# Softmax denominators of two head quads taken together, merged rows moved once a set, and later planned landings, in a scheduled transformer block

## The chip, the cores and the metric

One core of a Trainium2 chip runs the whole kernel. Times are device microseconds of that core, from unprofiled executions; the profile is of one further execution with the hardware profiler on. Engines are named as the profile names them: PE is TensorE (PEld its weight loads), DVE VectorE, ACT ScalarE, POOL GpSimd, SP SyncE, whose queue issues nearly all transfers.

## What is computed

A transformer block with conditioning: layer norm and modulation, attention with 32 heads of 16 dimensions over 2048 tokens, a residual, a second layer norm, and a GEGLU feed-forward network (FFN) with 1792 hidden columns.

```python
sa, ca, ga, sb, cb, gb = split(silu(c) @ w_mod, 6)        # six rows of 512
h = layernorm(x) * (1 + ca) + sa                          # x: 2048 x 512
q, k, v = heads(h @ wqkv)                                 # 32 heads of 16
p = softmax(q @ k.T * 16 ** -0.5)                         # 32 x 2048 x 2048
x = x + ga * (merge(p @ v) @ wo)
h = layernorm(x) * (1 + cb) + sb
x = x + gb * ((gelu(h @ w_gate) * (h @ w_up)) @ w_down)
```

## The kernel before

**Tiling.** The 2048 queries are cut into nine sets (`SETS`): seven of 256 rows and two of 128. The 32 heads are cut into eight quads of four. A unit is a quad with a set (the first two sets go together in the first four quads, the last two in their first four). For each unit the scores of four heads against all keys are made on TensorE in blocks of 128 x 512 in PSUM; ScalarE takes their exponential two or three blocks at a time (`E<-ps_sc`), and VectorE takes some of the blocks instead, by a bit trick (`dreg`, `kq`, `mreg`, `sq`). The weighted sums with V accumulate in `ps_pv`; V has one column of ones more, so the 17th row of each head is the softmax denominator.

**Denominators (`unit_end`).** When a unit's sums are complete, VectorE copies them to `osb`, one of four slots of 256 columns. Then a chain runs: a transfer gathers the four rows of denominators on 128 partitions (`den<-osb`), VectorE takes the reciprocal (`rden<-den`), a transfer stores it in DRAM (`scr_rec<-rden`), four transfers broadcast it to the partitions of the four heads (`rb<-scr_rec`), and VectorE multiplies (`onorm<-osb,rb`). A head fills 16 of the 32 partitions that its place in the quad has. For some pairs of quads (`MERGED`), four transfers then move the rows of the odd quad beside those of the even one (`onorm<-onorm`), so that one matmul of the output projection takes both. The quads 6 and 7 of the last two sets (and quad 5 of the last) take another way, over TensorE (`near_end`).

**The rest of the work.** Projections of later rows, the output projection (`side_wo`), the second layer norm and the FFN of sets that are done (`side_ffn`) are side work: `plan` gives each piece a start and a due position in the sequence of score blocks, and `stream` doles it out in proportion. The FFN's weights are loaded again for each of the first sets, in pieces of 256 KB through two buffers for the gate and up weights (names beginning with `st`; the down weights of those sets `sd`), and kept for the last ones (`wg`, `wu`, `wd`).

**What sets the order.** The program's order on each engine is fixed when it is built. `stream` walks through the score blocks with a model of each engine's time and picks at each step what the model takes to be ready. Engines then run in that order, so a wrong estimate shows as a wait in which everything behind it on the same engine stands. For a transfer the model takes an issue cost on SyncE (`ISSUE`, by the first letters of the transfer's name) and a landing time, to which `MARGIN` adds some nanoseconds: `db` is the gather, `dc` the store, `dd` the broadcasts, `de` the merges, `qo` the transfers that split queries of odd and even quads.

**Fillers.** When TensorE would be idle, `stream` puts in matmuls that have no use (`xs,ident`), if the columns that it streamed in the last 3413 ns are fewer than `FILL` (`short`):

```python
    def short(self, t):
        w = 0
        for s, k in reversed(self.log):
            if s < t - 3413:
                break
            w += k
        return FILL - w
```

**The tail.** After the last exponential (`tail`) come the projection and FFN of the last two sets.

Of the kernel before, what the change touches and what calls it, by code (L numbers as in the profile page):

```python
# [6 lines left out]
ALU = mybir.AluOpType  # L7
# [6 lines left out]
P = 128  # L14
# [3 lines left out]
DH = 16  # L18
# [4 lines left out]
NKT = S_TOK // P  # L23
VW = DH + 1
EPS = 1e-5
FILL = 4200
GELU_C = 0.044715
TANH_C0 = float(np.sqrt(2.0 / np.pi))

# [2 lines left out]
NSETS = len(SETS)  # L32
OCOL = (0, 256, 0, 256, 0, 256, 0, 256, 384)
# [15 lines left out]
FLOW = sum(a + n <= 1536 for a, n in SETS)  # L49
URGENT = 9  # L50
LATE = 2
ISSUE = {"dd": 462, "de": 630, "db": 610, "dc": 400, "st": 410, "sd": 530, "wu": 420, "wg": 510, "wd": 480, "ou": 400}
MARGIN = {"db": 1200, "dd": 1200, "de": 1200}
BACK = 6
GAP = 120
END = (0, None)
# [30 lines left out]
class _Recorder:  # L87
# [289 lines left out]
    def bn_aggr(self, out, in_):  # L377
        return self.rec("dve", lambda e: e.bn_aggr(out, in_), [in_], [out], cost=99)

    def dma(self, eng, out, in_, sem, noncontig=False):  # L380
        def fn(e):
            if noncontig:
                with self.nc.allow_non_contiguous_dma(reason="small strided transfer"):
                    return e.dma_start(out, in_)
            return e.dma_start(out, in_)  # L385
        n = mybir.dt.size(out.dtype)
        for _, k in out.ap:
            n *= int(k)
        run = min(int(a.ap[-1][1]) * mybir.dt.size(a.dtype) for a in (out, in_))
        return self.rec(eng, fn, [in_], [out], dma=sem, cost=(n, run, MARGIN.get(sem[:2], 0)))  # L390

    def emit(self, final):
        for s in self.count:
# [34 lines left out]
class _Kernel(_Recorder):  # L428
# [845 lines left out]
    def plan(self, ends, nsplit, begin):  # L1274

        def at(i):
            return i * 2.5 if i < nsplit / 2.5 else nsplit + 3 * (i - nsplit / 2.5)
        a = ends[0] + 33
        w = [(self.side_first, 0, at(30))]
        w.append((self.side_wo_load, at(30), at(30)))  # L1280
        w.append((lambda: self.side_dc(1), at(30), at(51)))
        w.append((self.side_mod, at(50), at(59)))
        w.append((self.scale_wo, at(59), at(59)))
        b, c = begin[2] - 12, begin[3] - 12
        w.append((lambda: self.side_dc(2), at(59), b))
        w.append((lambda: self.side_dc(3), b, c))
        for g in range(1, 4):
            w.append((lambda g=g: self.side_q_all(g), c + (a - c) * (g - 1) // 3, c + (a - c) * g // 3))
        n = ends[-1]
        m = NSETS - 2  # L1290
        for k in range(m):
            s0 = ends[k] + 33
            e = ends[m] - (20)
            if k < m - 1:
                e = max(ends[k + 1] + 30, ends[0] + 33 + (e - ends[0] - 33) * sum(SETS[k]) // SETS[m][0])
            w.append((lambda k=k: self.side_wo(k), s0, min(e, s0 + 15 * SETS[k][1] // P)))
            if k < m - 1:
                w.append((lambda k=k: self.side_ffn(k), s0, e))
            else:
                w.append((lambda k=k: self.turns(self.before_last(m), self.side_ffn(k)), s0, e))  # L1300
        k, s0 = NSETS - 2, ends[-2] - 16
        w.append((lambda: self.either(self.side_ffn(k, True), self.near_end(k + 1, 6, lambda: self.spare[2]), self.wo_last(k + 1), self.tail_rest(k, self.mi[:, :])), s0, n - 20))
        res = []
        for mk, s, e in w:
            self.dry = True
            tot = sum(y[0] for y in mk() if y is not None)
            self.dry = False
            res.append([mk(), s, e, tot, None])
        return res
# [31 lines left out]

    def short(self, t):

        w = 0
        for s, k in reversed(self.log):
            if s < t - 3413:
                break
            w += k
        return FILL - w

    def stream(self):
        self.split = True
# [8 lines left out]
        m = NSETS - 2  # L1361
# [9 lines left out]
        ends = [0] * NSETS  # L1371
# [13 lines left out]
        for u in units[2:]:  # L1385
            n, kpb = NKT * u[3] // 512, 512 // u[3]
            plain = list(range(T0 // kpb))
            m = len(plain) * 2 // 3
            for r in plain[:m] + list(range(len(plain), n)) + plain[m:]:
                add(u, r)  # L1390
        nseq = len(seq)
# [6 lines left out]
        pos = c = e = rp = loaded = 0  # L1398
# [28 lines left out]
        def pv(rnd, i, src):  # L1427
            u, r, g0 = rnd
            self.require([("v", r * (512 // u[3]) // 4, u[1] // 2)])
            self.pv_mms(rnd, acc_of(u), src, i, u not in begun, left[u] == 1)  # L1430
# [8 lines left out]
        def pv_next():  # L1439

            res = []
            for k in open_rounds():
                rnd = rounds[k]
                u, r, g0 = rnd
                if group[u] != cg or any(g0 + j not in self.slot for j in range(4)) or len(res) == 2:
                    break
                if left[u] == 1 and self.blocked(u):
                    break
                src = [self.slot[g0 + j] for j in range(4)]
                if ("v", r * (512 // u[3]) // 4, u[1] // 2) not in self.have:  # L1450
                    if tq is not None:
                        break
                    x = 0.0
                else:
                    x = self.probe(lambda: pv(rnd, 0, src))
                if res:
                    x = max(x, res[0][0])
                res.append((x, 0, k, rnd, 0, src, None))
                if left[u] <= 2:
                    break  # L1460
            n = 0
            for q in wait:
                u = q["rnd"][0]
                if group[u] != cg:
                    break
                for i, src in q["ready"]:
                    if n == 2 or (left[u] == 1 and self.blocked(u)) or (res and left[u] <= 2):
                        break
                    n += 1
                    res.append((self.probe(lambda: pv(q["rnd"], i, src)), 1, i, q["rnd"], i, src, q))  # L1470
            res.sort(key=lambda x: (max(x[0], t + 30), x[1]))
            return res

# [26 lines left out]
        while cg <= group[units[-1]]:  # L1500
# [7 lines left out]
            t = max(self.pe_now(), virt)  # L1508
# [168 lines left out]
    def unit_end(self, u, acc):  # L1677
        sets, qd, q0, W = u
        b, lo, hi = self.osb_span(u)
        osb, rb = self.osb[:, lo:hi], self.rb[:, lo:hi]  # L1680
        assert not self.blocked(u)
        self.copy("dve", osb, acc[:, 0:W])
        if sets[0] >= NSETS - 2 and len(sets) == 1 and qd >= (6 if sets[0] == NSETS - 2 else 5):
            self.done(("osb", sets[0], qd))
            return
        self.live[u] = (lo, hi)
        m = 4 * W // P
        o = 8 if BCOL[sets[0]] else 0
        sem = b + 4 * (o > 0)
        pair = (qd - 1, qd) in self.merged(sets[0])  # L1690
        s2 = self.scr2[b, P * o:P * o + 4 * W]
        den, rden = self.den[:, b, o:o + m], self.rden[:, b, o:o + m]
        steps = [
            ("sp", lambda: self.dma("sp", den, self.osb[DH:P:32, lo:hi].rearrange("j (a n) -> j a n", n=m), "db%d" % sem)),
            lambda: self.recip(rden, den),
            ("sp", lambda: self.dma("sp", s2.rearrange("(p n) -> p n", p=P), rden, "dc%d" % sem)),
            ]
        steps += [("sp", lambda j=j: self.dma(
            "sp", self.rb[32 * j:32 * j + DH, lo:hi],
            s2[W * j:W * j + W].rearrange("(o n) -> o n", o=1).broadcast_to([DH, W]), "dd%d%d" % (sem, j)))  # L1700
            for j in range(4)]

        def fin2():
            c = OCOL[sets[0]]
            self.tt("dve", self.onorm[:, qd, c:c + W], osb, rb, ALU.mult)
            if self.probing is None:
                self.live.pop(u)
                self.done(("half", u))
                if not pair:
                    for k in sets:  # L1710
                        self.done(("onorm", k, qd))

        def merge(j):
            c = OCOL[sets[0]]
            self.dma("sp", self.onorm[32 * j + DH:32 * j + 2 * DH, qd - 1, c:c + W], self.onorm[32 * j:32 * j + DH, qd, c:c + W],
                     "de%d%d" % (qd // 2, j))
            if self.probing is None and j == 3:
                for k in sets:
                    self.done(("onorm", k, qd))

        def free():
            c = OCOL[sets[0]]
            return ("den", u) in self.have and all(
                ("wo", k) in self.have for k in range(sets[0]) if OCOL[k] < c + W and c < OCOL[k] + SETS[k][1])
        self.task(steps, ("den", u))
        self.task([fin2], ("norm", u), free)
        if pair:
            self.task([("sp", lambda j=j: merge(j)) for j in range(4)], None,
                      self.after([("half", u)] + [("onorm", k, qd - 1) for k in sets]))


    def tail(self, ka, kb):

# [217 lines left out]
```

## Time and profile before

| | us |
|---|---|
| median of 3 runs | 832.73 (832.40 to 832.94) |
| the profiled execution | 841.73 |
| its span, first to last instruction | 840.0 |
| TensorE busy | 763.9 |
| VectorE busy | 727.4 |
| ScalarE busy | 793.3 |

The profiled execution is 9.0 us longer than the median. In the views that follow, a group's line gives line, engine, operation, the tiles written and read, shapes and count, then busy time, the mean of one in ns, and the idle time before it with what ended it. A line of the waits gives the total, the count and the longest. A line of the windows gives the stretch and its length, then for each engine shown the busy time and the count of instructions, then the granted TensorE clock, the share of the DMA engines and GB/s. A line of the timeline gives start and length, and in brackets the idle time before it. A line on a transfer of SyncE gives min, median and max of the issuing instruction in ns; one on transfers by size gives count, KB each and us to landing.

### The profile page before, as it was taken

What the parts mean: (1) busy time and instruction counts of PE and PEld (TensorE: products, weight loads), DVE (VectorE), ACT (ScalarE), POOL (GpSimd) and SP (SyncE); (2) the same over time, 40 slices, a digit from 0 to 9 for tenths busy, and PEclk for the clock granted to TensorE, in tenths of its full rate; (3) what the DMA queues carried; (4) which work ended last, traced back from release to release, by engine and by line L of the source; (5) the groups of instructions that cost most, each with busy time, mean ns of one, the idle gap of its engine ahead of it and who ended that gap; (6) DMA issues with size and microseconds to landing.
All of it is one profiled execution on the core that took longest, in us unless ns stands there. A gap on an engine that the chain in (4) does not pass through costs nothing.

```text
span 840.0 us, 37609 instructions
## 1 busy us (share of the span) xinstructions
PE 763.9 (91%) x17153; PEld 369.8 (44%) x17157; DVE 727.4 (87%) x1504; ACT 793.3 (94%) x746; POOL 4.5 (1%) x12
## 2 busy tenths in 40 slices
PE   8889999998899898989899899998998899999898
PEld 4333334343443354434444454344443443346567
DVE  7754878989899998899999998999997999989764
ACT  6999999999899998999999999999998999999782
POOL 1000000000000000000000000000000000000000
PEclk9999999999999999999999999999999999999899
DMA  9100000012540045114410541043234522200000
GB/s 303 44 14 11 12 9 18 8 23 72 148 133 23 11 135 139 32 28 126 134 42 17 148 125 39 16 124 111 59 86 114 166 73 65 64 12 11 14 13 13
DMA packets 105708, 57.40 MB, mean 68 GB/s; under 512 B 26701, under 2 KB 104782, under 8 KB 105550
## 3 DMA queue, kind: packets, MB, share of 16 engines
q1 hardware_dynamic: 105020, 54.48, 23.7%
q8 instruction: 134, 2.20, 1.1%
q10 hardware_dynamic: 530, 0.53, 0.2%
q14 instruction: 24, 0.20, 0.1%
HBM read 50.04 MB, written 2.35 MB: 62 GB/s over the span
## 4 chain that ended last, share of the span: by engine, by line
ACT 72%; PE 15%; DVE 5%; DMA 5%; SPq 2%; issue 1%; DVEq 0%
ACT E L335 70%; PE ps_sc L322 6%; PE ps_mi L322 6%; PE ps_pv L322 3%; SPq L385 2%; ACT wreg L335 2%; DMA scr_rec<-rden 2%; DMA rb<-scr_rec 2%; DVE mreg L347 1%; DMA xs<-in_B_w_down_dram 1%; DMA mreg<-in_B_w_gate_dram 1%; DVE wreg L339 0%; DMA mreg<-in_B_w_up_dram 0%; DVE wreg L356 0%; DVE onorm L339 0%
## 5 line engine op out<-in xcount | busy, mean ns | idle before, releaser
L335 ACT ACTIVATE E<-ps_sc 128x1024 bf16<-128x1024 f32 (+2 forms) x700 | 768.1, 1343 | 32.0 <-PE ps_sc L322 31.7
L322 PE MATMUL ps_sc<-qT,kT 32*128 32x256 bf16 (+3 forms) x2048 | 199.3, 275 | 25.5 <-ACT E L335 20.6
L322 PE MATMUL ps_sc<-qo,kT 32*128 32x256 bf16 (+2 forms) x2048 | 201.2, 275 | 19.5 <-ACT E L335 16.9
L322 PE MATMUL ps_pv<-E,vaug 128*17 128x256 bf16 (+2 forms) x3232 | 157.7, 275 | 1.9 <-DVE osb L356 1.2
L347 DVE TENSOR_SCALAR dreg<-ps_sc 128x512 uint16<-128x512 f32 x192 | 130.3, 685 | 15.4 <-PE ps_sc L322 13.7
L322 PE MATMUL ps_mi<-wreg,mreg 128*32 128x256 bf16 x2816 | 120.2, 279 | 7.3 <-DMA mreg<-in_B_w_up_dram 2.2
L322 PEld LDWEIGHTS ps_sc<-qT,kT 32*128 32x128 bf16 (+1 forms) x2048 | 61.3, 92 | 120.7 <-ACT E L335 100.3
L322 PEld LDWEIGHTS ps_sc<-qo,kT 32*128 32x128 bf16 x2048 | 61.5, 92 | 111.8 <-ACT E L335 99.1
L322 PEld LDWEIGHTS ps_pv<-E,vaug 128*17 128x17 bf16 x3232 | 61.8, 90 | 59.9 <-issue 41.8
L322 PEld LDWEIGHTS ps_mi<-wreg,mreg 128*32 128x32 bf16 x2816 | 65.0, 97 | 46.8 <-issue 24.2
L322 PE MATMUL ps_pv<-mreg,vs 128*17 128x256 bf16 (+2 forms) x1796 | 80.4, 272 | 3.5 <-DVE mreg L347 3.2
L347 DVE TENSOR_SCALAR mreg<-dreg 128x2048 uint16<-128x2048 uint16 x120 | 79.7, 681 | 0.1
L347 DVE TENSOR_SCALAR mreg<-ps_sc 128x512 uint16<-128x512 f32 x96 | 65.1, 685 | 8.7 <-PE ps_sc L322 7.9
L347 DVE TENSOR_SCALAR kq<-ps_sc 128x512 uint16<-128x512 f32 x96 | 65.2, 684 | 8.5 <-PE ps_sc L322 7.7
L322 PEld LDWEIGHTS ps_pv<-mreg,vs 128*17 128x17 bf16 x1796 | 39.4, 91 | 19.4 <-issue 6.9
L322 PE MATMUL ps_mi<-hreg,wreg 128*32 128x512 bf16 (+1 forms) x496 | 37.9, 377 | 1.0 <-DVE vaug L356 0.6
L352 DVE SCALAR_TENSOR_TENSOR wreg<-wreg,ps_mi 128x512 bf16<-128x512 bf16 x49 | 33.3, 679 | 3.3 <-PE ps_mi L322 2.6
L356 DVE CAST wreg<-ps_mi 128x512 bf16<-128x512 f32 x49 | 33.5, 684 | 1.9 <-PE ps_mi L322 1.0
L339 DVE TENSOR_TENSOR wreg<-wreg 128x1024 bf16<-128x1024 bf16 (+1 forms) x56 | 34.3, 613 | 0.0
L347 DVE TENSOR_SCALAR mreg<-kq 128x2048 uint16<-128x2048 uint16 x48 | 32.4, 684 | 0.7 <-PE ps_pv L322 0.7
L347 DVE TENSOR_SCALAR mreg<-mreg 128x2048 uint16<-128x2048 uint16 x48 | 32.6, 679 | 0.0
L339 DVE TENSOR_TENSOR onorm<-osb,rb 128x256 bf16<-128x256 f32 (+2 forms) x59 | 25.2, 428 | 6.1 <-DMA rb<-scr_rec 6.0
(171 smaller groups left out, 725.3 us busy)
## 6 DMA issues: line engine op xcount, KB each, us to landing
mreg<-in_B_w_up_dram SPq DMA_DIRECT2D x46, 256.0 KB, 3.1
mreg<-in_B_w_gate_dram SPq DMA_DIRECT2D x42, 256.0 KB, 3.4
dreg<-in_B_w_down_dram SPq DMA_DIRECT2D x18, 256.0 KB, 4.0
rb<-scr_rec SPq DMA_DIRECT2D x208, 16.0 KB, 1.8
mreg<-in_B_w_down_dram SPq DMA_DIRECT2D x12, 256.0 KB, 4.1
ereg<-in_B_w_down_dram SPq DMA_DIRECT2D x12, 256.0 KB, 3.4
mreg<-in_w_mod_dram SPq DMA_DIRECT2D x1, 2048.0 KB, 13.0
out_dram<-xs SPq DMA_DIRECT2D x15, 128.0 KB, 2.1
```

Source lines behind the costliest of these rows:

```text
L322: return self.rec("pe", lambda e: e.matmul(out, lhsT, rhs, start=start, stop=stop, tile_position=tp), [lhsT, rhs], [out], cost=(n, int(rhs ...
L335: return self.rec("act", lambda e: e.activation(out, in_, func, scale=scale, **kw), rd, wr, cost=self.cost("act", out, [in_], "act"))
L339: return self.rec(eng, lambda e: e.tensor_tensor(out, a, b, op), [a, b], [out], cost=self.cost(eng, out, [a, b], "tt"))
L347: return self.rec(eng, lambda e: e.tensor_scalar(out, a, s1, s2, **kw), rd, [out], cost=self.cost(eng, out, [a], "ts") + 60 * (len(rd) - 1 ...
L352: return self.rec("dve", lambda e: e.scalar_tensor_tensor(out, a, s, b, op0=op0, op1=op1), rd, [out], cost=self.cost("dve", out, [a, b], " ...
L356: return self.rec(eng, lambda e: e.tensor_copy(out, in_), [in_], [out], cost=self.cost(eng, out, [in_], "ts"))
L385: return e.dma_start(out, in_)
```

## The change

- Sets of 256 rows (and the joint unit of the last two): the even quad of each pair only copies its sums; after the odd one, one chain serves both, with 512 columns: one gather, one reciprocal with 16 columns in place of two with 8, one store, four broadcasts of 512, one multiply of 2 x 256. The first, 512 wide units stay as they were.
- The merges of all odd quads of a set go out together, in four transfers a set, when the last of them is multiplied.
- `MARGIN` is raised for most transfers, and a chain's transfers get a further `EARLY` in quads before 6 (1500 ns for the gather, 2500 for the broadcasts, 2000 for the merges). `qo` gets an issue cost of 620 in place of the default 450.
- `FILL` goes from 4200 to 3700. `HALF` and `SAFE` are 0 and change nothing.
- In `plan`, the due position of the FFN of the first seven sets is put 80 blocks later.

By the two programs' instruction order, TensorE goes from 17149 to 17032 instructions (111 fillers, and 6 where part of the last projection is no longer split in four), VectorE from 1506 to 1454, SyncE from 674 to 466, ScalarE stays at 748.

```diff
-FILL = 4200
+FILL = 3700
+HALF = 0
...
-ISSUE = {"dd": 462, "de": 630, "db": 610, "dc": 400, "st": 410, "sd": 530, "wu": 420, "wg": 510, "wd": 480, "ou": 400}
-MARGIN = {"db": 1200, "dd": 1200, "de": 1200}
+ISSUE = {"dd": 462, "de": 630, "db": 610, "dc": 400, "st": 410, "sd": 530, "wu": 420, "wg": 510, "wd": 480, "ou": 400, "qo": 620}
+SAFE = 0
+EARLY = (1500, 2500, 2000)
+MARGIN = {"db": 1200, "dd": 1800, "de": 1500, "qo": 1500, "st": 1500, "sd": 1700, "wd": 1700, "wu": 1500, "wg": 1500}
...
-        return self.rec(eng, fn, [in_], [out], dma=sem, cost=(n, run, MARGIN.get(sem[:2], 0)))
+        return self.rec(eng, fn, [in_], [out], dma=sem, cost=(n, run, MARGIN.get(sem[:2], 0) + late))
...
-            e = ends[m] - (20)
+            e = ends[m] + 60
...
-        return FILL - w
+        return max(FILL - w, HALF - h)
...
         self.live[u] = (lo, hi)
-        m = 4 * W // P
+        two = W == 256 and sets[0] < NSETS - 2 or len(sets) > 1 and sets[0]
+        if two and qd % 2 == 0:
+            return
+        us = [u]
+        if two:
+            us, lo, b = [(sets, qd - 1, q0, W), u], lo - W, b - 1
+        L = hi - lo
+        m = 4 * L // P
...
-        pair = (qd - 1, qd) in self.merged(sets[0])
-        s2 = self.scr2[b, P * o:P * o + 4 * W]
+        late = EARLY if qd < 6 else (0, 0, 0)
+        s2 = self.scr2[b, P * o:P * o + 4 * L]
...
-            s2[W * j:W * j + W].rearrange("(o n) -> o n", o=1).broadcast_to([DH, W]), "dd%d%d" % (sem, j)))
+            s2[L * j:L * j + L].rearrange("(o n) -> o n", o=1).broadcast_to([DH, L]), "dd%d%d" % (sem, j), late=late[1]))
...
-            self.tt("dve", self.onorm[:, qd, c:c + W], osb, rb, ALU.mult)
+            n = len(us)
+            self.tt("dve", self.onorm[:, qd + 1 - n:qd + 1, c:c + W], self.osb[:, lo:hi].rearrange("p (a n) -> p a n", a=n),
+                    self.rb[:, lo:hi].rearrange("p (a n) -> p a n", a=n), ALU.mult)
...
+        odd = [g[1] for g in self.merged(sets[0]) if len(g) == 2]
...
-            self.dma("sp", self.onorm[32 * j + DH:32 * j + 2 * DH, qd - 1, c:c + W], self.onorm[32 * j:32 * j + DH, qd, c:c + W],
-                     "de%d%d" % (qd // 2, j))
+            self.dma("sp", self.onorm[32 * j + DH:32 * j + 2 * DH, 0:2 * len(odd):2, c:c + W], self.onorm[32 * j:32 * j + DH, 1:2 * len(odd):2, c:c + W],
+                     "de%d" % j, late=late[2])
...
-        if pair:
+        if qd == odd[-1]:
             self.task([("sp", lambda j=j: merge(j)) for j in range(4)], None,
-                      self.after([("half", u)] + [("onorm", k, qd - 1) for k in sets]))
+                      self.after([("half", k, x) for k in sets for x in odd] + [("onorm", k, x - 1) for k in sets for x in odd]))
```

## What was predicted

> **What bounds the kernel now.** I read the page first: engines, then the chain that ended last.
>
> ```profile
> span 840.0 us, 37609 instructions
> PE 763.9 (91%) x17153; PEld 369.8 (44%) x17157; DVE 727.4 (87%) x1504; ACT 793.3 (94%) x746; POOL 4.5 (1%) x12
> ## 4 chain that ended last, share of the span: by engine, by line
> ACT 72%; PE 15%; DVE 5%; DMA 5%; SPq 2%; issue 1%; DVEq 0%
> ```
>
> ScalarE's exponentials set the pace: 72% of the chain, 94% busy. The change touches none of them; both programs hold 280 exponentials of 1536 columns, 412 of 1024 and 8 shorter ones. So the most that can be won is ScalarE's idle time. The stages, by ScalarE's busy time:
>
> ```profile
> 15.30:796.00 780.70, 760.16 (x704) 0.98 0.25 67
> 796.00:814.67 18.67, 18.59 (x15) 1.00 0.08 21
> 814.67:840.00 25.33, 7.02 (x14) 1.00 0.04 12
> ```
>
> Three numbers follow. Up to 796 us ScalarE idles 780.70 - 760.16 = 20.54 us; from there to its last exponential 0.08 us; and behind that lies a tail of 25.33 us in which it hardly works. I laid windows round the idle stretches that ScalarE's timeline shows in these 20.54 us and kept the eight behind which a transfer was late.
>
> ```profile
> 226.00:231.00 5.00, 1.89 (x3) 0.67 0.67 176
> sum 23.00, ACT 12.55; mean ACT 1.57
> 780.00:796.00 16.00, 10.30 (x10) 0.79 0.05 9
> ```
>
> The sum is that of the eight: 23.00 - 12.55 = **10.45 us** lost behind late transfers, 3.11 of it in the window shown. The other 10.09 us have no transfer behind them, 5.70 of it between 780 and 796. That the eight hang on transfers is in the view of waits:
>
> ```profile
> DVE onorm L339 <- DMA rb<-scr_rec: 6.0, 5, 2.4
> PE ps_mi L322 <- DMA mreg<-in_B_w_up_dram: 2.2, 1, 2.2
> DVE xs L339 <- DMA xs<-in_B_w_down_dram: 2.3, 3, 1.0
> DVE rden L359 <- DMA den<-osb: 1.8, 2, 1.2
> ```
>
> VectorE and TensorE take their work in order. When the multiply `onorm` stands 2.4 us before its broadcast, the score conversions queued behind it stand too, the matmuls that need the bank they free stand, and ScalarE runs dry. These waits are mistakes of the planner: it put the multiply where it took the broadcast to have landed.
>
> **The change part by part.**
>
> *Landings set later (MARGIN, EARLY, the qo issue cost).* The planner now takes the broadcast to land 0.6 us later than before, and 3.1 us later (0.6 + EARLY's 2.5) for quads 0 to 5; the gather 1.5 us later for those quads; staged up and gate weights 1.5; down weights 1.7. Against the longest waits: the 2.4 on a broadcast and the 1.2 on a gather are covered for three pairs of four, the 1.0 on down weights is covered, and of the 2.2 on up weights 0.7 stays. Other work fills the place, since only the waiting instruction moves back: VectorE's order now has a median of 20 instructions between reciprocal and multiply in place of 16, and never under 11 where it was 8. Bounds: 0, if waits only move, and -10.45. I take two thirds, **-7.0**, by the cover just counted.
>
> *Fewer transfers.* SyncE's queue is the other reason for lateness; what it issues waits in order too.
>
> ```profile
> L385 SPq DMA_DIRECT2D rb<-scr_rec x236: 302/420/3272, 73.9 to 806.8; - x118
> L385 SPq DMA_DIRECT2D onorm<-onorm x84: 522/589/1757, 90.5 to 784.3; - x84
> L385 SPq DMA_DIRECT2D den<-osb x59: 538/592/712, 68.1 to 799.4; - x59
> L385 SPq DMA_DIRECT2D scr_rec<-rden x59: 332/344/1177, 72.3 to 803.5; - x59
> SPq L385 <- DVE rden L359: 96.4, 33, 6.2
> rb<-scr_rec SPq DMA_DIRECT2D x208, 16.0 KB, 1.8
> rb<-scr_rec SPq DMA_DIRECT2D x16, 32.0 KB, 1.9
> ```
>
> SyncE loses 104 broadcasts, 52 merges, 26 gathers and 26 stores: 104 x 0.420 + 52 x 0.589 + 26 x 0.592 + 26 x 0.344 = 98.6 us of issuing out of 840. The waits for a reciprocal (96.4 us), in which weight loads and qo transfers stand in the queue, have half as many causes; and a broadcast of twice the size lands as soon (1.9 us for 1.8). None of that is on the chain except as earlier landings, so I add no term: it is what keeps the 7.0 from being given back.
>
> *Wider reciprocal and multiply.*
>
> ```profile
> L359 DVE RECIPROCAL rden<-den 128x8 f32<-128x8 f32 x52 | 10.0, 193 | 1.8 <-DMA den<-osb 1.8
> L359 DVE RECIPROCAL rden<-den 128x16 f32<-128x16 f32 x4 | 1.0, 243 | 0.0
> L339 DVE TENSOR_TENSOR onorm<-osb,rb 128x256 bf16<-128x256 f32 x52 | 21.7, 417 | 6.1 <-DMA rb<-scr_rec 6.0
> L339 DVE TENSOR_TENSOR onorm<-osb,rb 128x512 bf16<-128x512 f32 x4 | 2.7, 682 | 0.0
> ```
>
> Fifty-two of each become 26: 26 x (2 x 193 - 243) = 3.7 us and 26 x (2 x 417 - 682) = 4.0 us, so 7.7 us off VectorE. Ends: 0, and -7.7 if VectorE bound everywhere. It is 5% of the chain, so **-0.4**.
>
> *The even quad waits for the odd one.* Its slot in `osb` is held one quad longer.
>
> ```profile
> L356 DVE COPY osb<-ps_pv x63: 278/415/693, 67.4 to 815.9; 128x256 f32<-128x256 f32 x52, 128x128 f32<-128x128 f32 x8, 128x512 f32<-128x512 f32 x3
> 207.37 0.41 DVE L356 COPY osb<-ps_pv 128x256 f32<-128x256 f32 x1
> 225.33 0.43 DVE L339 TENSOR_TENSOR onorm<-osb,rb 128x256 bf16<-128x256 f32 x1 [2.42 <-DMA rb<-scr_rec]
> ```
>
> Copies come every (815.9 - 67.4) / 62 = 12.1 us. A slot is wanted again three quads (36 us) after the odd one's copy; the slowest chain in the table of waits took 225.33 - 207.37 = 18.0 us. Cost 0, under a cover of 18 us; past it, the last matmuls of quad 4 would hold TensorE. The merges of all three pairs now go out after quad 5; quads 6 and 7 still follow, 24 us, and the output projection waits for those anyway: 0.
>
> *Filler cut (FILL 4200 to 3700).* Fillers fall from 60 groups of four matmuls to 33 (the rows hold one group more, the start of the last projection).
>
> ```profile
> L322 PE MATMUL ps_sc<-xs,ident 128*32 128x512 bf16 x140 | 12.1, 397 | 4.2 <-ACT E L335 4.1
> L322 PE MATMUL ps_mi<-xs,ident 128*32 128x512 bf16 x104 | 9.2, 392 | 0.0
> core 0: 840.0 us, clock 0.986
> 46.80:50.20 3.40, 2.36 (x32) 1.08 (x31) 1.99 (x4) 3.40 (x4) 0.00 (x0) 1.00 0.03 7
> 50.20:53.60 3.40, 3.37 (x98) 1.70 (x95) 0.72 (x2) 3.40 (x4) 0.00 (x0) 1.00 0.00 0
> 449.60:453.00 3.40, 2.09 (x48) 0.68 (x44) 3.28 (x13) 3.40 (x4) 0.00 (x0) 1.00 0.06 11
> 453.00:456.40 3.40, 3.40 (x39) 0.95 (x34) 1.89 (x4) 2.66 (x3) 0.00 (x0) 0.50 0.12 15
> 695.30:698.70 3.40, 2.24 (x55) 0.75 (x48) 3.40 (x7) 3.40 (x5) 0.00 (x0) 1.00 0.51 136
> 698.70:702.10 3.40, 3.40 (x37) 0.79 (x38) 2.50 (x6) 2.62 (x3) 0.00 (x0) 0.51 0.59 163
> ```
>
> A group takes (12.1 + 9.2) / 61 = 0.35 us: 27 x 0.35 = 9.4 us off TensorE, which at 15% of the chain is -1.4. The price is in the windows, whose first figure is TensorE's busy time and whose third from the end is the granted clock. It halves for 3.4 us after a window in which TensorE was busy 2.09 or 2.24 us, and stays whole after one with 2.36. The mean of 0.986 makes 840 x 0.014 / 1.7 = seven halved windows. Those at 453 and 698 us follow a window in which ScalarE was full (3.40), so no stall caused them. A halved window costs ScalarE 3.40 - 2.66 = 0.74 us. One filler less would take the window at 46.8 from 2.36 to 2.01. I take three new ones: -1.4 + 2.2 = **+0.8**. Ends: -1.4, and +3.8 with seven new ones (5.2 - 1.4).
>
> Here a rule can be set against the rows. The Trainium skill, "TensorE: Matmul & The Clock Gate", section "Why this matters for your kernels", asks for no idle gap of TensorE over about 3 us between bursts of matmuls. By that, fillers could go freely, and the term would be -1.4. The trace disagrees: 2.09 us of work in 3.40 us was not enough.
>
> *Side work due 80 blocks later (plan).* In the new order the last transposes for set 7, their four modulations, the projection of three quads and two single-quad normalisations come behind or among the last weighted sums, ahead of the first tail matmul; before, these lay under the exponentials.
>
> ```profile
> L347 DVE TENSOR_SCALAR wreg<-ps_mi,modB 128x128 bf16<-128x128 bf16 x4 | 1.2, 339 | 1.3 <-PE ps_mi L326 1.3
> L356 DVE COPY rb<-rden 128x128 f32<-128x128 f32 x5 | 1.1, 225 | 0.1
> L339 DVE TENSOR_TENSOR onorm<-osb,ps_mi 128x128 bf16<-128x128 f32 x3 | 0.9, 285 | 1.7 <-PE ps_mi L322 1.7
> ```
>
> On VectorE that is 4 x 0.34 + 2 x (0.225 + 0.285) = 2.4 us at most; nothing if TensorE has tail work to hide it. Half: **+1.2**. In return the FFN is spread thinner over the middle, which I price at 0, as ScalarE's idle there had the causes above.
>
> Sum: -7.0 - 0.4 + 0.8 + 1.2 = -5.4. The profiled execution took 841.73 us (span 840.0 and 1.73 round it), so 836.3, or 0.9936 of it. The median of the runs is 832.73, 9.0 less than the profiled one, and 0.9936 of that is **827.4 us**.
>
> **The rivals.**
>
> A, the gate needs an empty window, as that rule has it: the filler term is -1.4, the sum -7.6, 825.2 us. Against it stand the two windows above. Chance 0.08.
>
> B, more than the landings: all 10.45 goes, and half of the 5.70 between 780 and 796: -10.45 - 2.85 - 0.4 + 0.8 + 1.2 = -11.7, 821.2. For it: the queue is 98.6 us lighter. Against: the rest has causes that the diff does not name. Chance 0.10.
>
> C, the waits move. The order is another one throughout, and its new tight places are where no margin was measured; only 1.5 of the 7.0 remains, which the filler and the tail eat (-1.5 - 0.4 + 0.8 + 1.2 = +0.1): 832.8. For it: five waits on broadcasts among 59 chains are few, and a new order can draw five others. Chance 0.13.
>
> D, slower, by the clock gate. With fillers aimed lower, any short wait takes a lean window under 2.3 us of work; the halving makes scores late, and what hangs on them makes the next window lean. The sum without new halvings is -5.4 - 2.2 = -7.6, so it decides from the eleventh new one (11 x 0.74 = 8.1). With fifteen: -7.6 + 11.1 = +3.5, 836.2. For it: 0.12 us separates the leanest harmless window from a harmful one, against 0.35 for a filler. Against: the planner still fills up to 3700 columns in each 3413 ns, and of 27 groups gone eleven would have to come out of windows near the edge. Chance 0.23.
>
> **How the numbers follow.** Forecast 0.46, A 0.08, B 0.10, C 0.13, D 0.23. The likeliest is 827.4, whose own range is 823 to 831 by the ends of its first term and the tail. The three runs lie within 0.06%; a change of under 0.2% (1.7 us) I call the same. So faster 0.46 + 0.08 + 0.10 = 0.64, same 0.13, slower 0.23. The range from 820.5 to 836.5 takes in B and the middle of D.
>
> **What would show it.** Right: the waits of `onorm` on its broadcast fall from 6.0 us to under 2 and those on up and down weights to under 1; ScalarE's idle up to its last exponential falls from 20.6 to some 13 to 15 us; the halved windows number four to eight; the stretch behind the last exponential grows from 25.3 to 26 or 27. If that stretch is unchanged, the tail term was wrong; if the halvings pass fifteen, D. The forecast is wrong outright if ScalarE idles as long with the transfer waits gone: then these waits were not what starved it.

## The result, and the profile after

| | before | after |
|---|---|---|
| median, first comparison (5 runs each) | 832.94 (832.40 to 836.21) | 826.26 (825.94 to 828.30) |
| ratio, 95% interval | | 0.9913 (0.9889 to 0.9937) |
| the profiled execution | 841.73 | 828.30 |
| its span | 840.0 | 826.5 |

The kernel is 6.7 us faster in the median. Three of before's five runs are those that stood ahead of the prediction, the other two took 835.23 and 836.21; after's five take in its profiled execution, its longest. The profiled executions lie 13.4 us apart; that difference is taken up below. First the page of after: span, engines and the chain that ended last.

```profile
span 826.5 us, 37027 instructions
PE 753.5 (91%) x17040; PEld 366.2 (44%) x17040; DVE 722.6 (87%) x1452; ACT 792.4 (96%) x746; POOL 4.5 (1%) x12
## 4 chain that ended last, share of the span: by engine, by line
ACT 84%; PE 15%; DVE 1%; issue 1%
```

Transfers and SyncE's queue, 5% and 2% of the chain before, are gone from it, and ScalarE has taken their place: 84% where it had 72%. Its busy time is the same (792.4 for 793.3). The view of waits of after has two waits on transfers, one of them at the start and in both kernels, the other 0.4 us of a weight load, which before has too:

```profile
DVE st L378 <- DMA xs<-in_A_x_dram: 1.5, 2, 1.0
PEld ps_mi L325 <- DMA mreg<-in_B_w_gate_dram: 0.4, 1, 0.4
```

So the waits quoted with the prediction, and two of 0.8 us that it did not quote, 13.9 us in all, came to nothing. ScalarE's windows of after, from its second exponential to the last and from there to the end (columns: stretch, length, ScalarE's busy time and count, clock, share of the DMA engines, GB/s), and the stretch in which before lost 5.70 us of its 16:

```profile
15.57:800.11 784.54, 777.71 (x719) 0.99 0.24 67
800.11:826.54 26.43, 7.13 (x13) 0.98 0.05 14
764.00:780.00 16.00, 14.68 (x14) 1.00 0.08 14
```

ScalarE now idles 784.54 - 777.71 = 6.83 us in the stream, where it idled 20.6; the stretch behind the last exponential is 26.43 us, where it was 25.33; the hard place near the end costs 1.32 us in place of 5.70. Then SyncE's issues, and VectorE's groups:

```profile
L388 SPq DMA_DIRECT2D rb<-scr_rec x132: 302/420/2458, 77.8 to 792.9; - x132
L388 SPq DMA_DIRECT2D onorm<-onorm x32: 588/616/1719, 167.2 to 773.9; - x32
```

```profile
L342 DVE TENSOR_TENSOR onorm<-osb,rb 128x512 bf16<-128x512 f32 x30 | 20.4, 681 | 0.0
L362 DVE RECIPROCAL rden<-den 128x16 f32<-128x16 f32 x30 | 7.3, 242 | 0.0
```

A broadcast's issue costs what it did (420 ns), a merge's 616 ns for 589, and there are fewer; multiply and reciprocal last 681 and 242 ns, as the rows of before had them (682, 243), and the 6.0 us of idle time before the multiply are 0.0.

### The profile page after: what moved, and what is told of

Its sections match the earlier page's. It is cut to its first block, busy times and chain, and to the rows that moved or that the text cites. A ratio compares the mean times of both kernels' runs of the same rounds, so it can differ in the third digit from the quotient of the medians.

```text
span 826.5 us, 37027 instructions
## 1 busy us (share of the span) xinstructions
PE 753.5 (91%) x17040; PEld 366.2 (44%) x17040; DVE 722.6 (87%) x1452; ACT 792.4 (96%) x746; POOL 4.5 (1%) x12
## 4 chain that ended last, share of the span: by engine, by line
ACT 84%; PE 15%; DVE 1%; issue 1%
ACT E L338 81%; PE ps_sc L325 6%; PE ps_mi L325 5%; PE ps_pv L325 3%; ACT wreg L338 3%; PE ps_mi L329 0%; DVE mreg L350 0%; DVE xs L342 0%; DVE wreg L342 0%; DVE wreg L355 0%; PE ps_sc L329 0%; DVE wreg L350 0%; ACT hreg L338 0%; DVE osb L359 0%; DVE kT L359 0%
## 5 line engine op out<-in xcount | busy, mean ns | idle before, releaser
L325 PE MATMUL ps_sc<-qT,kT 32*128 32x256 bf16 (+3 forms) x2048 | 202.3, 275 | 26.7 <-ACT E L338 22.6
L325 PE MATMUL ps_sc<-qo,kT 32*128 32x256 bf16 (+2 forms) x2048 | 197.5, 274 | 27.1 <-ACT E L338 24.8
L350 DVE TENSOR_SCALAR dreg<-ps_sc 128x512 uint16<-128x512 f32 x192 | 130.4, 685 | 13.9 <-PE ps_sc L325 13.2
L325 PE MATMUL ps_mi<-wreg,mreg 128*32 128x256 bf16 x2816 | 117.0, 277 | 4.2 <-DVE wreg L355 2.1
L338 ACT ACTIVATE wreg<-wreg 128x1024 bf16<-128x1024 bf16 (+1 forms) x28 | 31.1, 1111 | 0.0
```

The source lines that it names most:

```text
L325: return self.rec("pe", lambda e: e.matmul(out, lhsT, rhs, start=start, stop=stop, tile_position=tp), [lhsT, rhs], [out], cost=(n, int(rhs ...
L338: return self.rec("act", lambda e: e.activation(out, in_, func, scale=scale, **kw), rd, wr, cost=self.cost("act", out, [in_], "act"))
L350: return self.rec(eng, lambda e: e.tensor_scalar(out, a, s1, s2, **kw), rd, [out], cost=self.cost(eng, out, [a], "ts") + 60 * (len(rd) - 1 ...
```

## The experiments

Three theories were set against each other. M: late transfers cost the time, and planning them later cures it. P: the lighter queue cures it. L: any other order draws other waits, and this one drew few. From the second set on, T: ScalarE's idle time comes from late transfers and halved windows, and what the plan leaves over lengthens the stretch behind. Each set of four ran on one chip beside runs of before of its own, whose median was 838.14, 839.04 and 836.21 us; so kernels are compared by their ratio, and best within a set. In the table the ratios are of all executions and the rest is from the one profiled execution of each: idle is ScalarE's idle time from its second exponential to the last, stretch what follows, waits the sum of those of VectorE and of TensorE's matmuls on transfers behind the start, halved the number of windows of 3.4 us at half clock before the last exponential, in the trace's record of the clock.

| kernel | ratio to before (95%) | idle | stretch | waits | clock | halved |
|---|---|---|---|---|---|---|
| before | 1 | 20.6 | 25.3 | 13.9 | 0.986 | 7 |
| after | 0.9913 (0.9889 to 0.9937) | 6.8 | 26.4 | 0 | 0.989 | 5 |
| m_alone | 0.9985 (0.9962 to 1.0008) | 10.6 | 29.1 | 4.3 | 0.994 | 3 |
| p_alone | 0.9939 (0.9916 to 0.9961) | 11.4 | 26.0 | 2.7 | 0.994 | 3 |
| no_margin | 0.9967 (0.9943 to 0.9991) | 16.7 | 28.6 | 12.7 | 0.988 | 6 |
| fill_4200 | 0.9927 (0.9901 to 0.9953) | 6.0 | 31.4 | 0 | 0.998 | 1 |
| p_and_m | 0.9964 (0.9940 to 0.9988) | 14.0 | 31.0 | 2.7 | 0.990 | 5 |
| due_20 | 0.9870 (0.9838 to 0.9902) | 8.9 | 29.2 | 2.7 | 0.992 | 4 |
| fill_3600 | 0.9858 (0.9829 to 0.9886) | 6.8 | 26.2 | 1.1 | 0.996 | 2 |
| fill_3000 | 0.9994 (0.9965 to 1.0022) | 13.8 | 29.5 | 0.9 | 0.988 | 6 |
| after_again | 0.9893 (0.9866 to 0.9920) | 3.3 | 27.0 | 0.2 | 0.998 | 1 |
| due_70 | 0.9965 (0.9943 to 0.9988) | 10.7 | 29.0 | 2.7 | 0.986 | 7 |
| fill_3900 | 0.9880 (0.9850 to 0.9909) | 4.6 | 25.7 | 1.4 | 1.000 | 0 |
| bcast_600 | 0.9929 (0.9903 to 0.9955) | 14.5 | 27.0 | 1.3 | 0.984 | 8 |

One profile need not be typical of its kernel: those of bcast_600 (837.22 us of 827.03 to 837.22), due_70 (835.03 of 829.18 to 836.48) and p_and_m (839.13 of 834.18 to 839.19) are among the longest executions of theirs.

### One part at a time

**m_alone**: before with the later landings and the issue cost of `qo` (its line is left out here).

```diff
-MARGIN = {"db": 1200, "dd": 1200, "de": 1200}
+EARLY = (1500, 2500, 2000)
+MARGIN = {"db": 1200, "dd": 1800, "de": 1500, "qo": 1500, "st": 1500, "sd": 1700, "wd": 1700, "wu": 1500, "wg": 1500}
...
+        late = EARLY if qd < 6 else (0, 0, 0)
```

> The kernel before with the later landings alone (MARGIN, EARLY on each chain of its own quad, the qo issue cost). Theory M (the late transfers cost the time, and planning them later cures it): 825 to 829 us, at least 4 us under before; the waits of VectorE and TensorE on transfers, some 13 us in all before, fall under 2 us. Theory P (the lighter queue cures it): 831 to 835 us, waits on broadcasts stay above 3 us. Theory L (any other order draws other waits): anywhere from 826 to 838, waits on transfers 5 to 15 us.

Ratio 0.9985, an interval that takes in 1, so no gain in time is shown; on 832.94 it makes 831.7, in P's band (831 to 835). Its waits on transfers, and its windows as above:

```profile
PE ps_mi L323 <- DMA mreg<-in_B_w_up_dram: 2.9, 3, 2.3
DVE rden L360 <- DMA den<-osb: 1.2, 2, 0.7
DVE onorm L340 <- DMA rb<-scr_rec: 0.2, 1, 0.2
```

```profile
16.17:806.55 790.38, 779.80 (x719) 0.99 0.24 66
806.55:835.67 29.12, 7.13 (x13) 1.00 0.05 16
```

M is half right. Waits fell from 13.9 to 4.3 us, where M had under 2, those on broadcasts from 6.0 to 0.2, where P had over 3, and idle fell by 10.0 us (790.38 - 779.80 = 10.58). But the stretch behind grew by 3.8, the start by 0.9 and ScalarE's busy time in the stream by 1: of 10 us won in the stream, 4.3 are left in the span of the profiled execution. The expectation had no place for a longer stretch. In this order the last weighted sums, the transposes of set 7 and their normalisations come late: the tail's first FFN matmul starts 6.1 us behind the last exponential, in after 3.4.

**p_alone**: after with the old `FILL`, due position, `MARGIN` and `ISSUE`, and `EARLY` zero, that is the pairing and the merges once a set alone.

> The kernel before with the pairing and the merges once a set alone; old landings, filler aim and due position. Theory P: 825 to 829 us, SyncE issues 466 transfers in place of 674, waits on transfers fall under half (6 us). Theory M: 831 to 835 us, waits on transfers stay above 8 us, as the multiply is still planned where the broadcast is late. Theory L: anywhere from 826 to 838.

Ratio 0.9939: on the 832.94 that the expectation assumed it makes 827.9, in P's band (in its own set, 832.66 beside 838.14). The waits:

```profile
DVE onorm L342 <- DMA rb<-scr_rec: 2.0, 2, 1.7
PE ps_mi L325 <- DMA mreg<-in_B_w_gate_dram: 0.7, 1, 0.7
```

2.7 us with the old landings: P's number, against M's. Idle fell by 9.2, and the stretch stayed near 26. Whether the lighter queue did that, or the order that this kernel happened to draw, the next run asks.

**no_margin**: after with the old landings and the default issue cost of `qo`.

```diff
...
-EARLY = (1500, 2500, 2000)
-MARGIN = {"db": 1200, "dd": 1800, "de": 1500, "qo": 1500, "st": 1500, "sd": 1700, "wd": 1700, "wu": 1500, "wg": 1500}
+EARLY = (0, 0, 0)
+MARGIN = {"db": 1200, "dd": 1200, "de": 1200}
```

> The kernel after with the old landings (MARGIN as before, EARLY zero, qo at the default issue cost). Theory M: the waits on transfers come back (over 6 us) and the time goes up by 4 us or more, to 830 to 834. Theory P: stays at 826 to 828. Theory L: moves by several us either way with waits on transfers that do not follow it.

```profile
PE ps_mi L325 <- DMA mreg<-in_B_w_gate_dram: 4.1, 6, 1.2
PE ps_mi L325 <- DMA mreg<-in_B_w_up_dram: 3.7, 2, 2.2
DVE onorm L342 <- DMA rb<-scr_rec: 2.3, 2, 1.8
DVE rden L362 <- DMA den<-osb: 2.0, 2, 1.5
```

As M says, the waits come back (12.7 us with 0.6 on down weights), idle to 16.7, and 0.9967 is 0.0054 or 4.5 us above after, by ratios of two sets; on 832.94 it makes 830.2, in M's band. Its stretch (28.6) is 2.1 us longer than after's, with ten matmuls of the last FFN matrix for set 6 left over in it. It has p_alone's pairs and landings, with other fillers and another due position, and nearly five times its waits: with the old landings the number of waits is a matter of the order drawn. With the later ones it is less so: every kernel that has them had 4.3 us of waits at most, after itself none by this count, where the three with the old ones had 13.9, 2.7 and 12.7.

**p_and_m**: after with `FILL = 4200` and the old due position.

> The kernel after with the old filler aim (4200) and the old due position: the pairing and the later landings together. In its instruction order two row tiles of the FFN of set 6 (ps_mi<-xs,hreg and ps_mi<-hreg) have not been placed when the scores end. Theory T (the landings win about 10 us before the last exponential, and what is left over of the side work lengthens the stretch behind it by some 2.7 us a tile): idle up to the last exponential 6 to 9 us, stretch behind it 30 to 33 us, ratio to before 0.990 to 0.996. Theory S (the parts simply add: -1.3 us and -5.1 us by the runs of each alone): idle 9 to 12 us, stretch 25 to 29, ratio 0.992.

Ratio 0.9964. Theory S, that parts add, falls: 0.9939 and 0.9985 would have made 0.9924. Theory T had the stretch (31.0) and all but the ratio (its band ends at 0.996), but not the idle time of 14.0. Its one wait on a transfer was the longest of all:

```profile
DVE onorm L342 <- DMA rb<-scr_rec: 2.7, 1, 2.7
```

The landings do not cover every wait, and a good part of these 14 us has no wait on a transfer beside it. 3.7 us of them lie inside the five halved windows; the rest I did not trace to one cause.

### The fillers and the gate

**fill_4200**: after with `FILL = 4200`.

> The kernel after with the old filler aim of 4200. By the prediction's filler term (-1.4 for TensorE's time, +2.2 for new halved windows) it should come out 0.8 us faster than after, with 2 or 3 halved windows fewer in the profile; by the rule that only an empty window throttles, 1.4 us slower with as many halved windows. Theory L: 2 us or more either way.

Idle was 6.0 us for 6.8, the granted clock of the profile 0.998 for 0.989. Over all executions the two differ less: 0.997 in the mean here, 0.994 for after's first five and 0.995 for after_again's six. The kernel was no faster than after (0.9927 for 0.9913, intervals that overlap), and its stretch was 31.42 us, so neither the 0.8 nor the 1.4 us of the expectation is settled. TensorE's timeline says what lies in it:

```profile
797.30:828.72 31.42, 7.13 (x13) 1.00 0.06 18
```

```profile
800.68 2.54 PE L325 MATMUL ps_mi<-xs,hreg 128*128 128x512 bf16 x11 [0.25 <-DVE wreg L350]
803.06 0.59 PE L325 MATMUL ps_mi<-hreg 128*128 128x512 bf16 x2
```

Thirteen matmuls of the last FFN matrix for one row tile of set 6 come 3.4 us behind the last exponential. The planner had not placed them earlier, and the tail's own matmuls wait behind these 3.0 us (800.68 to 803.65).

**fill_3000**: after with `FILL = 3000`, 15 groups of fillers in place of 33.

> The kernel after with a filler aim of 3000: 15 groups of fillers in place of 33, one row tile left over. If a window of TensorE needs some 2.3 us of 3.4 busy (the prediction), the halved windows go from about 6 to 12 or more, at 0.74 us each: 4 us more idle before the last exponential, ratio 0.996 or more with the tile left over. By the rule that only an idle gap of some 3 us throttles: halved windows as in after, idle 6 to 8 us, ratio 0.994.

Ratio 0.9994: the whole gain is gone, with waits on transfers of 0.9 us. Its stretch (29.5 us) is 3.1 us longer than after's, with eight matmuls of the row tile left over in it. Most of the rest, I take it, is the clock. This execution has a clock of 0.988, but it is one of the better: over its twelve executions the granted clock was 0.976 to 0.994, 0.983 in the mean, against 0.990 to 0.998, 0.995 in the mean, for the six of after_again. At 1.7 us of clock lost for each halved window that is 8 windows for 2 or 3. Three windows of TensorE that each stood directly before a halved one, and the first halved one:

```profile
30.50:33.90 3.40, 2.02 (x23) 0.48 (x19) 3.16 (x13) 3.40 (x4) 0.00 (x0) 1.00 0.02 5
47.60:51.00 3.40, 2.06 (x26) 0.85 (x24) 1.84 (x4) 3.40 (x4) 0.00 (x0) 0.99 0.01 2
371.80:375.20 3.40, 2.20 (x47) 0.88 (x46) 2.65 (x11) 3.40 (x4) 0.00 (x0) 1.00 0.05 7
34.00:37.40 3.40, 3.40 (x25) 1.13 (x25) 2.13 (x6) 3.03 (x3) 0.00 (x0) 0.51 0.00 0
```

They held 2.02, 2.06 and 2.20 us of work, none near empty. The prediction's reading of the gate, that a window needs work and not only the absence of a gap, holds, if not as a sharp limit (below); the count of halved windows in the one profile (6) missed the 12 expected, and only the clocks of all executions show the rise. The executions of one kernel show the price too: fill_3000 took 832.38 us at a clock of 0.994 and 843.26, 840.19 and 838.82 at 0.976, that is nine more windows for 6.4 to 10.9 us, some 0.7 to 1.2 us each. A straight line through time against halved windows ((1 - clock) x span / 1.7) rises 1.5 us a window over the executions of before in each of the three sets, an estimate from 73 of them: more than the 0.74 us that a halved window takes from ScalarE, as what brings the halving, or follows it, is in it too. From 3600 up the aim hardly moves the clock: its mean is 0.996 for fill_3600, 0.995 for after_again, 0.997 for fill_3900 and fill_4200.

**fill_3600**: after with `FILL = 3600`.

> The kernel after with a filler aim of 3600 in place of 3700: 35 groups of fillers in place of 33, and nothing left over behind the scores. Theory T: stretch 26 to 27 us, idle 6 to 9 us, ratio to before within 0.002 of that of after (0.989 to 0.993). Theory L (the gain is the luck of one order): several us slower, with idle before the last exponential back above 12 us.

0.9858, idle 6.8, stretch 26.2: T's numbers, with a ratio 0.003 below T's band. Against L: a neighbour of after, with another order and nothing left over behind the scores, is as fast as after. bcast_600, below, is another such neighbour and is slower, so one of them does not settle it.

### The stretch behind the last exponential

**due_20**: after with `e = ends[m] - 20`. One row tile is left over.

> The kernel after with the old due position of the side work. One row tile is left over behind the scores in its order. The prediction's tail term says the later due position costs 1.2 us, so this should be 1.2 us faster than after, with a stretch of 25 us. Theory T: the stretch is 28 to 29 us, and the run 1 to 3 us slower than after (ratio 0.993 to 0.995), with no waits on transfers either way.

The stretch was 29.18 us, as T had it; the prediction's 25 was wrong. But the ratio of 0.9870 is not the slower one that T expected: after was not in this set, fill_3600 beside it had 0.9858, and the intervals overlap. It had 2.7 us of waits on transfers, where T had none. A stretch 3 us longer than fill_3600's went with a time that can't be told from it.

**due_70**: after with `e = ends[m] + 70`, one row tile left over, beside after_again.

> The kernel after with the due position of the side work 10 blocks later still (70 in place of 60). Its order leaves one row tile of the FFN of set 6 (13 matmuls of 512 columns) behind the scores. Theory T: stretch 28.5 to 30 us, idle as in after, so 2 to 3 us slower than after beside it. If the tile hides behind the normalisations of the tail: stretch 26 to 27, time as after.

```profile
804.28:833.30 29.02, 7.13 (x14) 1.00 0.05 15
PE ps_mi L325 <- DMA mreg<-in_B_w_up_dram: 1.8, 1, 1.8
DVE rden L362 <- DMA den<-osb: 0.9, 1, 0.9
```

The first line is of its windows, the others of its waits. The stretch has its 2.1 us over after_again, so the tile is not hidden. The median is 831.88 for 825.82, 6.1 us slower, where 2 to 3 were expected: waits on up weights and gather came back and the clock fell, to 0.986 in the profile and 0.990 in the mean of twelve executions (0.995 for after_again), for ten blocks of 2000 in a due position.

**after_again**: after, unchanged.

> The kernel after, unchanged, beside three neighbours on one chip. Theory T (idle up to the last exponential by late transfers and halved windows, then the stretch behind it by what is left over): idle 6 to 9 us, no waits on transfers over 1 us, stretch 26 to 27 us, ratio 0.986 to 0.993. Theory L (one lucky execution): idle above 10 us.

```profile
15.77:795.85 780.08, 776.74 (x719) 1.00 0.24 67
795.85:822.80 26.95, 7.13 (x14) 1.00 0.04 13
```

0.9893, within the first interval; 825.82 us for 826.26. Idle is 3.34 us at a clock of 0.998, half of the first profile's and below T's 6 to 9. The program is the same, and in the first one the clock was halved in five windows of the stream where here it was in one.

**fill_3900**: after with `FILL = 3900`, nothing left over and the last transposes earlier. **bcast_600**: `FILL = 3600`, gather and broadcast taken to land 0.6 us later again.

> The kernel after with a filler aim of 3900: 60 groups of fillers in place of 33, nothing left over, and the last transposes of set 7 sixteen steps before the last weighted sum, where after has them behind it. Theory T: stretch 24.5 to 25.5 us, at most 3 halved windows, idle 6 to 8 us: 1 to 2 us faster than after. If fillers are in TensorE's way (the -1.4 of the prediction's filler term): idle 8 to 10 us and no faster.

> The kernel after with a filler aim of 3600 and the gather and broadcast taken to land another 0.6 us later; nothing left over. Theory T: the waits that fill_3600 still had on gather and broadcast (1.0 us) go, idle 6 to 7 us, stretch 26 to 27.5: within 1 us of fill_3600 and of after. Theory L: several us off.

```profile
15.44:795.39 779.95, 775.34 (x719) 1.00 0.24 68
795.39:821.10 25.71, 7.13 (x14) 1.00 0.05 17
core 0: 821.1 us, clock 1.000
```

fill_3900 has the shortest span of all, 821.1 us, with a whole clock and a stretch 1.2 us under after_again's. Its median, 824.28 for 825.82, has a ratio of 0.9880 for 0.9893, whose intervals overlap: a likely gain, not a shown one. Idle was 4.6 us, so with 60 groups of fillers in place of 33 nothing shows that they are in TensorE's way. bcast_600 missed: 0.9929, a clock of 0.984 and idle of 14.5 us, 6.2 of them in eight halved windows, with 1.3 us of waits, none of them on gather or broadcast. Its median is 4.6 us over after_again's. More slack for two transfers took their waits away and made it no faster than its neighbours, and slower in this draw.

## Why the prediction was right

The time, 826.26, lies 1.1 us from 827.4. Two errors cancel in that, so its nearness is in part luck. By its steps:

- **Landings, -7.0, too small.** All of the 10.45 us went: of waits on transfers 0.4 us is left, and waits and idle time fell together in m_alone, after, fill_4200 and fill_3600 (p_and_m and bcast_600, with idle of 14.0 and 14.5 us beside few waits, are exceptions). The two thirds came from counting which waits the later landings cover. The 10.45 was not the price of the waits alone: three of before's seven halved windows (from 227.7, 326.7 and 644.1 us) fall in those eight stretches, each behind a late transfer. In all, 9.8 of before's 20.6 us of idle time lie in halved windows, 3.0 of after's 6.8. And SyncE's queue was lighter as well; I had it add nothing. p_alone idled 9.2 us less by the pairs alone, as much as m_alone by the landings alone (10.0), but no_margin, with the same pairs and the same old landings, only 3.9 less. So what the lighter queue does by itself is not shown.
- **The other 10.09 us of idle time, priced at 0.** After has 6.83 us of idle time of every kind. The stretch between 780 and 796, which I left to rival B, went from 5.70 to 1.32 us; in before it holds two halved windows (784.1 to 790.9 us) behind a stand of TensorE of 2.4 us, in after a stand of 1.5 us and a whole clock. The stream of the profiled pair fared as B said: B's sum was -11.7, the span fell by 13.5.
- **Fewer transfers, no term.** The queue's waits for a reciprocal fell from 96.4 to 74.9 us, not by half. The wide broadcast took 2.3 us to land in the median of after, 2.0 in after_again and 1.9 in p_alone, where I read 1.9; the longest of all broadcasts took 3.9 us, where before had 5.3.
- **From the profiled execution to the median.** This is the step that failed and was saved by the others. I carried the sum over in proportion. The profiled execution of before was 9.0 us above its median, that of after 2.0. Before runs from 831.6 to 845.2 us over the three later sets, and its profiled execution, with seven halved windows and a 2.4 us stall of TensorE, was one of its long ones. A sum of -13.4 for the profiled pair is -6.7 in the medians of that comparison and -10.4 in those of the last set (836.21 and 825.82). Had I sized the first two steps right, I would have forecast too fast a kernel. The noise was misjudged with it: I took three runs within 0.06% for it, and the 73 later executions of before spread over 1.6%. Much of that spread goes with the clock, and so does part of the gain: at the same granted clock, in the last set, before took 832.89 to 836.24 us and after_again 826.64 and 827.75 (0.992), or 831.61 and 824.54 to 824.99 (0.998). Some 7 us are left at the same clock; the rest of the 10.4 is a clock that was halved less often (0.991 in the mean for before, 0.995 for after_again).
- **VectorE, -0.4.** Not seen by itself. Its operations have the durations that were used, and busy time fell from 727.4 to 722.6, by 4.8 us of the 7.7 counted.
- **The even quad's wait, 0.** No run shows a hold-up at the slots of `osb`.
- **Fillers, +0.8.** The price of a window was right in kind: 6.80 - 5.47 and 10.20 - 8.49 us over five windows of after make 0.6 us each, for 0.74. The -1.4 for TensorE's own time is not seen: fill_3900 has 27 groups more and idles less. Windows of after and, last, of before:

```profile
47.30:54.10 6.80, 6.73 (x49) 2.18 (x49) 1.80 (x4) 5.47 (x6) 0.00 (x0) 0.50 0.01 2
456.90:467.10 10.20, 10.14 (x132) 3.72 (x134) 6.11 (x12) 8.49 (x8) 0.00 (x0) 0.50 0.18 52
43.90:47.30 3.40, 2.17 (x23) 0.83 (x21) 2.43 (x8) 3.40 (x4) 0.00 (x0) 1.00 0.01 2
453.50:456.90 3.40, 2.41 (x43) 0.88 (x42) 1.92 (x7) 3.40 (x4) 0.00 (x0) 1.00 0.00 0
661.17:664.58 3.41, 2.08 (x55) 1.08 (x54) 2.59 (x6) 3.41 (x4) 0.00 (x0) 1.00 0.61 184
```

  The first two are halved stretches of after, the next two the windows that stand before them. Of the three new halvings the one that I had named came: in all five profiles with an aim of 3700 the window before 47 us holds 2.1 to 2.3 us of work (2.17 above, 2.36 in before) and is followed by one or two halved windows; in no profile with an aim of 3600, 3900 or 4200 is the clock halved there, so a lower aim need not bring it. The count fell all the same, from seven to five and one, as those behind late transfers went. And there is no sharp limit, as I drew it: 2.41 us of work was followed by a halving here, and 2.08 in before (last line) was not. The rule of the Trainium skill, "TensorE: Matmul & The Clock Gate", section "Why this matters for your kernels", asks only that gaps stay under about 3 us; the trace does not bear out that this is enough, here or in fill_3000. In the streams of all fourteen profiles TensorE never stood longer than 2.4 us, and the clock was halved in 58 windows.
- **The tail, +1.2.** The stretch grew by 1.1 us (25.33 to 26.43), and by 1.6 in after_again. The size was right, the reason only in part. I charged the later due position; due_20 puts it back and has 29.2 us. What counts is what the order leaves behind the scores. A row tile of set 6 left over goes with 2 to 5 us more stretch: due_70 has one and 2.1 us over after_again, fill_4200 one and 5.0 over after, p_and_m two and 4.5; no_margin, due_20 and fill_3000 have eight to ten matmuls of one, and 28.6 to 29.5 us. In m_alone (29.1) the last transposes come 1.4 to 3.6 us behind the last exponential, in after within 1.0. Kernels with neither, after, fill_3600, fill_3900 and bcast_600 among them, have 25.7 to 27.0. It is not all lost time, as due_20 shows.

Of the rivals, A falls with fill_3000, though its 825.2 us lies as near the result as the forecast. D's mechanism is there, in fill_3000, and at 3700 in the window before 47 us alone. C, that waits move, is what p_and_m, due_20 and due_70 show, with 2.7 us of waits each, and after escaped it. One place is tight whatever the draw: the eighth multiply, near 235 us, waited for its broadcast in seven of the twelve profiles of kernels with pairs, for 0.2 to 2.7 us, and in after that broadcast landed only some 0.4 us ahead of it.

What stays open: how much of the gain belongs to landings and how much to pairs. Either takes some 10 us out of the stream alone, both took 13.8 in after and only 6.6 in p_and_m; each edit redraws the whole order, and with one draw of each the parts can't be told apart better. The nine programs that have both parts lie between 0.9858 and 0.9994 of before: that the change is faster is shown, but how much is as much a matter of the order drawn as of the parts.

## What to carry to other kernels

In a kernel whose order is fixed by a planner, a wait on a late transfer can cost more than itself, through what stands behind it in order and then a halved clock: 2.4 us of wait at 225 us of before went with 3.11 us of ScalarE's idle time. Over the whole stream it cost less than itself, 10.45 us for 13.9. Look for those waits in the trace and set the planned landing by the latest seen rather than the usual one; no_margin shows what goes back when that is undone. Taking transfers out of the queue that carries them may help too, but one draw of p_alone and one of no_margin disagree. Compare such edits over several executions and several neighbouring settings, with the clock of each beside its time, and by the stretches of the span apart (start, stream, end). Of 10 us won in m_alone's stream 3.8 were given back at the end, and in fill_4200 thirteen matmuls that no longer fitted stand in an end that is 5.0 us longer.

## What was not expected of the hardware

TensorE stood still near the end of most profiled executions with nothing in the trace that released it, between 758 and 810 us, where matmuls are half as wide and come faster. Before and after (view of waits, TensorE):

```profile
PE ps_mi L322 <- issue: 2.4, 1, 2.4
```

```profile
PE ps_pv L325 <- issue: 1.7, 2, 1.5
```

The longest was 2.4 us in before, 0.9 to 2.0 in ten others, and under 0.8 in due_70, fill_3900 and bcast_600. What makes it was not tried. And one program differs from itself by the clock: after was profiled with five halved windows in the stream and, another time, with one, and idled 6.8 and 3.3 us.
